# Six of 32 pieces of float64 weights narrowed during the retention, the other 26 with planned earliest times

## The chip, the core and the metric

The kernel runs on one core of a Trainium2 chip. The metric is the device time of one execution in microseconds (us). The engines are TensorE (PE, with its weight loads shown apart as PEld), VectorE (DVE), ScalarE (ACT), GpSimd (POOL) and SyncE (SP), which only issues transfers here. ACT and POOL issue some transfers too; their queues are named SPq, ACTq and POOLq.

## The reference

Three layers follow each other. Only what matters here is shown:

```python
scores = scale * np.matmul(q, k.transpose(0, 1, 3, 2))
ret = scores * Dmat[None, :, :, :]          # decays, causal
attn = np.matmul(ret, v)                    # 4 x 8 heads, 576 positions, 64 wide
# x: 2304 tokens x 512. 8 experts of 288 tokens each, filled in order of the logits
order = np.argsort(-flat)
h = np.maximum(x[mask] @ w1[e], 0.0)
out[mask] = h @ w2[e]
# last layer: 512 -> 2048 -> 512
h = x @ w_in
g = h * np.tanh(softplus(h))
return g @ w_out
```

`w_in` and `w_out` arrive as float64, since they are scaled by a float64 number. [...]

## The kernel before

**Retention (lines 133 to 304).** The 2304 tokens are worked through in 18 tiles of 128 (t = 0 to 17). In turn t of the loop at line 276 the program issues `load(t + 3)` (`qk` and `kv`, 512 KB each, line 168 and 170), `scale(t + 3)` on POOL (`ks`, `qs`, line 181 and 185), `scores(t + 1)` on PE (line 195) with its masking on DVE (`am`, line 198), then for tile t `carried` (line 223) and `outputs` (line 232) on PE into the PSUM tile `pT`, whose two halves ACT copies to `xT` (line 236), `state` (line 209, then DVE line 212), and `turn(t - 1)`: four matmuls into `pX` (line 246), a reduction on DVE (line 248), two ACT copies to `xs` (line 250) and a store (line 252). `pT` and `pX` share one tag with two buffers (line 216 and 243). They alternate, so that all `pT` tiles lie in one buffer and all `pX` tiles in the other: `carried(t + 1)` can't begin before `xT(t)` is copied out, nor `turn(t)` before `xs(t - 1)` is. The order of PE, DVE and POOL is that of the code (`manual_schedule`, line 147). The order of ACT and of SP's transfers in this part is chosen by the framework's scheduler. Loads have five buffers each.

**Routing and experts (lines 376 to 858).** Eight rounds follow. In each, DVE and PE find the 288 tokens of one expert bit by bit (`G`, `small`, lines 434 to 477), POOL gathers their rows (`xg`, line 613), PE transposes them (`mmx`, line 634), ACT and DVE split them into a high and a low part (`xh`, `xl`), and PE multiplies (`mma` and `mmb`, line 777). The weights come through five staging buffers (`st`) and are split likewise (`whi` on ACT, line 564; `wlo` on POOL or DVE, line 567). All this is recorded by a planner of the kernel's own (`run_tasks`, line 675): each task names an engine, a guessed duration, the events that it waits for and a priority (a smaller number goes first), and the planner writes the instructions down in the order in which they would start by its guesses.

**Narrowing (lines 705 to 767).** It is one of these planned tasks. There are 32 pieces (n = 0 to 31, 16 each of `w_in` and `w_out`), each of 128 x 512 float64 words (512 KB). Piece n is loaded into `std`; ACT scales the high words into `words` (line 741); DVE shifts (line 743) and joins low and high words into `dw` (line 746); ACT takes the sign into `dt` (line 750) and issues the store of piece n - 1 and the load of piece n + 3; POOL multiplies by the sign (line 760). Its priority is that of line 642: low (4) as long as the pieces are ahead of a plan that begins at `START` and allows `PACE` ns each, high (`UP`, 1.5) when they are behind it or when the eighth expert's tokens have been asked for (`URGENT`).

**Last layer (lines 860 to 1079).** The narrowed weights are read back (`final_units`), and six tiles of 384 tokens go through `hidden` (`mmc`, line 999), `gate` (sigmoid on ACT, two products and a reciprocal `q` on DVE, line 1029) and `outer` (`po`, line 1060).

Of the kernel before, what the change touches and what calls it, by code (L numbers as in the profile page):

```python
# [7 lines left out]
F32 = mybir.dt.float32  # L8
# [3 lines left out]
U32 = mybir.dt.uint32  # L12
# [13 lines left out]
NT = N // P  # L26
HP = H // 2
WARM = 11
STRADDLE = (4, 13)

GB = 96
# [21 lines left out]
NARROW_AT = (0, 0)  # L53
FIRST_UNITS = 2
EID = -2
PACE = 8000
START = 50000
WARM_TOOK = 215
WARM_N = 512
WARM_FROM = "tokens"  # L60
# [68 lines left out]
class Kernel:  # L129
# [3 lines left out]
    def attention(self):  # L133
# [8 lines left out]
        with ExitStack() as st:  # L142
            ld = st.enter_context(tc.tile_pool(name="ld", bufs=5))
            wk = st.enter_context(tc.tile_pool(name="wk", bufs=3))
            one = st.enter_context(tc.tile_pool(name="one", bufs=1))
            ps = st.enter_context(tc.tile_pool(name="ps", bufs=1, space=PSUM))
            st.enter_context(tc.manual_schedule(engines={mybir.EngineType.PE, mybir.EngineType.DVE, mybir.EngineType.Pool}))
            dec = one.tile([P, DCN], F32, name="dec")
# [26 lines left out]
            def scale(t, eng):  # L175

                if t >= NT:
                    return
                if not starts(t + 1):
                    KS[t] = wk.tile([P, H, D], F32, name="ks")  # L180
                    eng.tensor_tensor(KS[t], KV[t][:, 0], gks[:, t, :, None].to_broadcast([P, H, D]), op=ALU.mult)
                if not starts(t):
                    n = 64 if t in STRADDLE else P
                    QS[t] = QZ[t] if t in STRADDLE else wk.tile([P, HP, P], F32, name="qs")
                    eng.tensor_tensor(QS[t][:, :, :n], QK[t][:, 0, :, :n], gqs.rearrange("p (h i) -> p h i", i=P)[:, :, :n], op=ALU.mult)

            def scores(t):
                if t >= NT:
                    return
                pA = [ps.tile([P, HP, P], F32, name=f"pA{i}", tag="pA", bufs=2) for i in range(2)]  # L190
                for hp in range(HP):
                    for i in range(2):
                        sl = slice(i * 64, i * 64 + 64)
                        for o in (slice(0, 64), slice(64, P)):
                            nc.tensor.matmul(pA[i][o, hp, :], QK[t][sl, 1, hp, o], QK[t][sl, 0, hp, :], start=True, stop=True)
                AM[t] = wk.tile([P, 2, HP, P], F32, name="am")
                for i in range(2):
                    nc.vector.tensor_tensor(AM[t][:, i], pA[i], masks[t in STRADDLE][:, i], op=ALU.mult)

# [76 lines left out]
            for t in range(NT - 1):  # L276
                load(t + 3)
                scale(t + 3, nc.gpsimd)
                scores(t + 1)
                carried(t, Sb[seen[0] % 2])  # L280
                outputs(t)
                state(t)
                turn(t - 1)
                if t == 6:
                    self.routing_consts()
            t = NT - 1
            carried(t, Sb[seen[0] % 2])
            outputs(t)
            turn(t - 1)
            self.psum = lambda name, shape: ps.tile(shape, F32, name=name, tag="pS" if name == "pF" else "pA", bufs=1 if name == "pF" else 2)  # L290
            G = self.marks_of()
            self.chosen = self.rw.tile([GB, E, 3], I32, name="chosen", bufs=1)
# [346 lines left out]
        self.tasks.append([next(task), task])  # L639

    def narrow_priority(self):
        return UP if len(self.features) >= URGENT or len(self.narrowed) * PACE + START < self.time.get(PE, 0) else 4

    def arrival(self, n, at, wait=DMA_WAIT):
        self.time["dma"] = max(self.time.get("dma", 0), at.t) + n / DMA_RATE
# [53 lines left out]
    def step(self, t, done):  # L699
        try:  # L700
            t[0] = t[1].send(done)
        except StopIteration:
            self.tasks.remove(t)

    def narrow(self):

        nc, v, ic, a = self.nc, self.nc.vector, self.ic, self.a
        done = {k: {} for k in ("load", "read", "turn", "shift", "sign", "store")}

        def at(k, n):  # L710
            return [lambda: done[k].get(n)] if n >= 0 else []

        name = ("w_in", "w_out")
        words, sent = {}, {}

        def place(n):
            c, r = divmod(n // 2, a[name[n % 2]].shape[0] // P)
            return name[n % 2], slice(r * P, r * P + P), c

        def fetch(n, queue):  # L720
            if n < 32:
                w, r, c = place(n)
                words[n] = self.conv.tile([P, 512, 2], U32, name="std", bufs=3)
                queue.dma_start(words[n].rearrange("p c w -> p (c w)"), a[w].bitcast(U32)[r, c * 1024:c * 1024 + 1024])

        def send(n, queue):
            if n >= 0:
                w, r, c = place(n)
                queue.dma_start(a[w + "32"][r, c * 512:c * 512 + 512], sent.pop(n))

        def load():
            now = yield SP, 3 * DMA_ISSUE, [Event(0)], self.narrow_priority
            for n in range(3):
                fetch(n, nc.sync)
                self.spawn(piece(n, self.arrival(524288, now, LATE)))

        def piece(n, now):
            st, w = words[n], self.words.bitcast(U32)
            high = st[:, :, 1].bitcast(F32)
            now = yield ACT, 680, [now, *at("shift", n - 1)], self.narrow_priority  # L740
            nc.scalar.activation(self.words, high, AF.Copy, scale=2.0 ** -112)
            now = yield DVE, 620, [now], self.narrow_priority
            v.tensor_scalar(w, w, ic[:, IC["three"]], None, op0=ALU.logical_shift_left)
            now = yield DVE, 680, [now, *at("store", n - 4)], self.narrow_priority
            out = self.conv.tile([P, 512], U32, name="dw", bufs=4)
            v.scalar_tensor_tensor(out, st[:, :, 0], ic[:, IC["low"]], w, op0=ALU.logical_shift_right, op1=ALU.bitwise_or)
            done["shift"][n] = now
            sign = yield ACT, 800, [now, *at("sign", n - 1), *at("turn", n - 1)], self.narrow_priority
            t = self.conv.tile([P, 512], F32, name="dt", bufs=1)
            nc.scalar.sign(t, high)  # L750
            done["turn"][n] = sign
            send(n - 1, nc.scalar)
            fetch(n + 3, nc.scalar)
            if n:
                self.narrowed[n - 1] = done["store"][n - 1] = self.arrival(262144, sign, LATE)
            if n + 3 < 32:
                self.spawn(piece(n + 3, self.arrival(524288, sign, LATE)))
            now = yield POOL, 1310, [now, sign], self.narrow_priority
            sent[n] = out = out.bitcast(F32)
            nc.gpsimd.tensor_tensor(out, out, t, op=ALU.mult)  # L760
            done["sign"][n] = now
            if n == 31:
                now = yield SP, DMA_ISSUE, [now], self.narrow_priority
                send(n, nc.sync)
                self.narrowed[n] = self.arrival(262144, now)

        self.spawn(load())
# [354 lines left out]
```

## Time and profile before

| | |
|---|---|
| median of 3 runs | 800.22 us (799.56 to 802.0) |
| the profiled execution | 795.55 us, its span 793.8 us |
| PE busy | 752.2 us (95%) |
| PEld busy | 680.9 us (86%) |
| DVE, ACT, POOL busy | 670.7 (84%), 407.9 (51%), 484.1 us (61%) |
| moved by DMA | 112.53 MB, 142 GB/s mean |

A time is that of a whole execution; the span is the stretch of the profiled one in which instructions ran, and times in the rows below count from its start. Busy shares are means over stages with different limits: the retention ends at about 84 us, the experts at about 362 us, the last layer with the span.

### The profile page before, as it was taken

The numbers are of one execution on the slowest core, as the hardware profiler recorded it, in microseconds if no ns is written. First come the engines' busy times: TensorE is split into PE (matmuls) and PEld (weight loads), VectorE is DVE, ScalarE is ACT, GpSimd is POOL, SyncE is SP. The second block draws the span as 40 slices with busy tenths as digits, with TensorE's granted clock in tenths as the row PEclk, the third lists the DMA queues.
The fourth block names the chain that finished last, engine by engine and source line by source line (L and its number), as shares of the span: only waits on it lengthen the run. The fifth ranks groups of instructions, "written<-read, shape, count | busy, mean of one in ns | idle before, by whom it ended". The sixth has DMA issues, their size and how long they took to land.

```text
span 793.8 us, 16149 instructions
## 1 busy us (share of the span) xinstructions
PE 752.2 (95%) x6180; PEld 680.9 (86%) x6184; DVE 670.7 (84%) x1079; ACT 407.9 (51%) x781; POOL 484.1 (61%) x408
## 2 busy tenths in 40 slices
PE   6999469999999999799999999999999999999996
PEld 5888338999998999799999889789989989988995
DVE  2444687889889898777999999999999998999993
ACT  1233114557566575757765544564555555555452
POOL 5644035679797797430577565666657566666554
PEclk9999779999999999999999999999999999999999
DMA  9994156889888898986500010010001001000001
GB/s 341 408 338 156 54 172 204 268 286 305 268 285 297 277 308 252 349 287 205 178 20 21 1 46 15 21 40 21 13 8 51 10 20 41 21 1 22 19 1 40
DMA packets 61261, 112.53 MB, mean 142 GB/s; under 512 B 4864, under 2 KB 33152, under 8 KB 61184
## 3 DMA queue, kind: packets, MB, share of 16 engines
q1 hardware_dynamic: 44960, 74.01, 27.0%
q10 hardware_dynamic: 13248, 28.06, 10.3%
q0 software_dynamic: 2976, 9.44, 3.6%
q8 instruction: 48, 0.79, 0.4%
q14 instruction: 29, 0.24, 0.1%
HBM read 88.94 MB, written 22.54 MB: 140 GB/s over the span
## 4 chain that ended last, share of the span: by engine, by line
PE 42%; DVE 15%; ACT 2%; DMA 2%; POOL 2%; issue 1%; POOLq 0%; ACTq 0%; SPq 0%; DVEq 0%
PE po L1060 18%; PE mmc L999 17%; DVE q L1029 8%; PE mma L777 4%; DVE n L1024 4%; PE mmb L777 3%; DVE n L1034 1%; DMA st<-w 1%; ACT whi L564 1%; POOL n L1031 1%; DMA yt<-y_scratch 1%; DVE wlo L567 1%; POOL gl L1041 1%; POOL yl L959 0%; ACT q L1020 0%
## 5 line engine op out<-in xcount | busy, mean ns | idle before, releaser
L1029 DVE RECIPROCAL q<-q 128x384 f32<-128x384 f32 x96 | 243.9, 2541 | 4.7 <-ACT q L1027 4.6
L1031 POOL TENSOR_TENSOR n<-n,q 128x384 f32<-128x384 f32 x96 | 100.9, 1051 | 164.9 <-DVE q L1029 152.2
L567 POOL TENSOR_TENSOR wlo<-st,whi 128x1024 fp32r<-128x1024 f32 x51 | 122.7, 2419 | 15.7 <-ACT whi L564 11.6
L999 PE MATMUL mmc<-yl,whi 128*128 128x384 f32 x384 | 130.0, 338 | 2.1 <-POOL yl L959 2.0
L999 PE MATMUL mmc<-yh,whi 128*128 128x384 f32 x384 | 130.5, 340 | 0.1
L999 PE MATMUL mmc<-yh,wlo 128*128 128x384 f32 x384 | 129.9, 338 | 0.0
L1041 POOL TENSOR_TENSOR gl<-n,gh 128x384 fp32r<-128x384 f32 x96 | 118.6, 1239 | 7.0 <-ACT gh L1039 6.9
L1024 DVE SCALAR_TENSOR_TENSOR n<-s 128x384 f32<-128x384 f32 x96 | 113.6, 1184 | 3.7 <-POOL gl L1041 3.5
L1060 PE MATMUL po<-wlo,gh 128*128 128x512 f32 x288 | 115.6, 401 | 0.0
L1060 PE MATMUL po<-whi,gh 128*128 128x512 f32 x288 | 115.0, 399 | 0.0
L1060 PE MATMUL po<-whi,gl 128*128 128x512 f32 x288 | 114.0, 396 | 0.3 <-POOL gl L1041 0.3
L1039 ACT CAST gh<-n 128x384 fp32r<-128x384 f32 x96 | 49.3, 514 | 122.3 <-DVE n L1034 111.7
L564 ACT CAST whi<-st 128x1024 fp32r<-128x1024 f32 x80 | 82.9, 1045 | 33.8 <-DMA st<-w 27.8
L777 PE MATMUL mma<-xh,whi 128*128 128x288 f32 x256 | 78.0, 305 | 3.4 <-ACT xh L624 2.6
L777 PE MATMUL mma<-xl,whi 128*128 128x288 f32 x256 | 76.9, 301 | 1.9 <-DVE xl L626 1.9
L999 PEld LDWEIGHTS mmc<-yl,whi 128*128 128x128 f32 x384 | 72.1, 188 | 7.0 <-POOL yl L959 2.6
L777 PE MATMUL mmb<-hl,whi 128*128 128x288 f32 x256 | 77.3, 302 | 0.0
L777 PE MATMUL mmb<-hh,whi 128*128 128x288 f32 x256 | 77.2, 302 | 0.0
L777 PE MATMUL mma<-xh,wlo 128*128 128x288 f32 x256 | 76.6, 299 | 0.0
L999 PEld LDWEIGHTS mmc<-yh,whi 128*128 128x128 f32 x384 | 72.1, 188 | 4.8 <-ACT yh L956 0.3
L777 PE MATMUL mmb<-hh,wlo 128*128 128x288 f32 x256 | 75.8, 296 | 0.0
L999 PEld LDWEIGHTS mmc<-yh,wlo 128*128 128x128 f32 x384 | 72.0, 187 | 0.0
(149 smaller groups left out, 1522.3 us busy)
## 6 DMA issues: line engine op xcount, KB each, us to landing
st<-w SPq DMA_DIRECT2D x64, 512.0 KB, 6.1
qk<-qk SPq DMA_DIRECT2D x18, 512.0 KB, 8.1
kv<-kv SPq DMA_DIRECT2D x18, 512.0 KB, 6.6
std<-w_out ACTq DMA_DIRECT2D x15, 512.0 KB, 5.4
std<-w_in ACTq DMA_DIRECT2D x14, 512.0 KB, 5.4
x_scratch<-xs SPq DMA_DIRECT2D x18, 256.0 KB, 4.5
y_scratch<-y ACTq DMA_DIRECT2D x32, 144.0 KB, 4.3
yt<-y_scratch SPq DMA_DIRECT2D x22, 192.0 KB, 2.4
```

The lines of the kernel that those rows point to most:

```text
L564: self.nc.scalar.copy(dst[0], st)
L567: (self.nc.vector if lo.engine == DVE else self.nc.gpsimd).tensor_tensor(dst[1], st, dst[0].bitcast(F32), op=ALU.subtract)
L777: self.nc.tensor.matmul(bank[1][:, :CAP], al if h == 2 else ah, bl if h == 1 else bh, start=(first and j == h == 0), stop=(last and j == n ...
L999: self.nc.tensor.matmul(bank[1][:, :TILE], (wl if h == 2 else wh)[:, c, cs], x[c][h == 1], start=(c == h == 0), stop=(c == HP - 1 and h == 2))
L1024: v.scalar_tensor_tensor(u, s, 2.0, s, op0=ALU.subtract, op1=ALU.mult)
L1029: v.reciprocal(q, q)
L1031: nc.gpsimd.tensor_tensor(u, u, q, op=ALU.mult)
L1034: v.tensor_tensor(u, u, p, op=ALU.mult)
L1039: nc.scalar.copy(gh, u)
L1041: nc.gpsimd.tensor_tensor(gl, u, gh.bitcast(F32), op=ALU.subtract)
L1060: nc.tensor.matmul(po[j], (gl if h == 2 else gh)[:, js], (wl if h == 1 else wh)[:, f % 2], start=(f == h == 0), stop=(f == DFF // P - 1 an ...
```

## The change

Six pieces leave the planned narrowing and are written into the loop of the retention, in four steps per piece: its load, its shift (ACT, then DVE), its join (DVE, ACT for the sign, POOL for the product) and its store. By the code, piece n is loaded in turn n + 8, shifted in turn n + 10, joined in turn n + 11 and stored in turn n + 12. They have a pool of their own (`early`), in which `est`, the loaded piece, has three buffers and lies in SBUF as `ewords` does. The other 26 pieces stay in the planner, with a pace of 12000 instead of 8000 and a start at 45000 instead of 50000, and each now has an earliest planned time as well, which falls away with the eighth expert's request.

```diff
@@ constants
+EARLY_PIECES = 6
+PIECES_AT = 10
...
-PACE = 8000
-START = 50000
+PACE = 12000
+START = 45000
@@ attention
             one = st.enter_context(tc.tile_pool(name="one", bufs=1))
+            load_piece, shift_piece, join_piece, store_piece = self.early_pieces(st.enter_context(tc.tile_pool(name="early", bufs=1)))
...
             for t in range(NT - 1):
                 load(t + 3)
                 scale(t + 3, nc.gpsimd)
+                load_piece(t - PIECES_AT + 2)
                 scores(t + 1)
+                join_piece(t - PIECES_AT - 1)
                 carried(t, Sb[seen[0] % 2])
                 outputs(t)
                 state(t)
                 turn(t - 1)
+                shift_piece(t - PIECES_AT)
+                store_piece(t - PIECES_AT - 2)
...
             turn(t - 1)
+            for n in range(t - PIECES_AT - 2, EARLY_PIECES):
+                store_piece(n)
@@ narrow_priority
-        return UP if len(self.features) >= URGENT or len(self.narrowed) * PACE + START < self.time.get(PE, 0) else 4
+        return UP if len(self.features) >= URGENT or (len(self.narrowed) - EARLY_PIECES + 1) * PACE + START < self.time.get(PE, 0) else 4
@@ new
+    def early_pieces(self, pool):
+        nc, v = self.nc, self.nc.vector
+        st, words, out = {}, {}, {}
+        def load(n):
+            st[n] = pool.tile([P, 512, 2], U32, name="est", bufs=3)
+            nc.sync.dma_start(st[n].rearrange("p c w -> p (c w)"), self.piece_of(n)[0])
+        def shift(n):
+            words[n] = pool.tile([P, 512], F32, name="ewords", bufs=2)
+            nc.scalar.activation(words[n], st[n][:, :, 1].bitcast(F32), AF.Copy, scale=2.0 ** -112)
+            w = words[n].bitcast(U32)
+            v.tensor_scalar(w, w, self.ic[:, IC["three"]], None, op0=ALU.logical_shift_left)
+        def join(n):
+            out[n] = pool.tile([P, 512], U32, name="edw", bufs=3)
+            v.scalar_tensor_tensor(out[n], st[n][:, :, 0], self.ic[:, IC["low"]], words[n].bitcast(U32),
+                                   op0=ALU.logical_shift_right, op1=ALU.bitwise_or)
+            t = pool.tile([P, 512], F32, name="edt", bufs=2)
+            nc.scalar.sign(t, st[n][:, :, 1].bitcast(F32))
+            out[n] = out[n].bitcast(F32)
+            nc.gpsimd.tensor_tensor(out[n], out[n], t, op=ALU.mult)
+        def store(n):
+            nc.sync.dma_start(self.piece_of(n)[1], out[n])
...
@@ narrow
+        begin = EARLY_PIECES
+        for n in range(begin):
+            self.narrowed[n] = Event(0)
...
-            for n in range(3):
+            for n in range(begin, begin + 3):
...
         def piece(n, now):
...
-            now = yield ACT, 680, [now, *at("shift", n - 1)], self.narrow_priority
+            turn = lambda: Event(0 if len(self.features) >= URGENT else (n - begin) * PACE + START)
+            now = yield ACT, 680, [now, turn, *at("shift", n - 1)], self.narrow_priority
```

The instructions stand as follows. **ACT, start of the retention**, from the first `xT` on, before (tiles 0 and 1 make the `x4`):

```order
L236 COPY xT<-pT 128x256 x4
L250 COPY xs<-pX 128x4x64 x2
L236 COPY xT<-pT 128x256 x2
L250 COPY xs<-pX 128x4x64 x2
L236 COPY xT<-pT 128x256 x2
```

and with the change (lines 239 and 253 are the copies, 733 and 742 the two ACT steps of a piece):

```order
L239 COPY xT<-pT 128x256 x2
L733 ACTIVATE ewords<-est 128x512
L742 ACTIVATE edt<-est 128x512
L239 COPY xT<-pT 128x256 x2
L733 ACTIVATE ewords<-est 128x512
L742 ACTIVATE edt<-est 128x512
L253 COPY xs<-pX 128x4x64 x2
L239 COPY xT<-pT 128x256 x2
```

Both ACT steps of piece 0 now stand between the copies of tile 0 and of tile 1, and those of piece 1 ahead of the first `xs`. The ACT steps of pieces 2 to 5 stand much later, each ahead of an `xT` between tiles 11 and 14 or just behind it.

**SP, the transfers behind the fourth `kv`**, before (the `x2` are `qk` of tiles 5 and 6):

```order
L337 DMA rc<-rconsts 128x211
L339 DMA ic<-iconsts 128x194
L168 DMA qk<-qk 128x1024 x2
L170 DMA kv<-kv 128x1024
L168 DMA qk<-qk 128x1024
```

and with the change:

```order
L346 DMA rc<-rconsts 128x211
L348 DMA ic<-iconsts 128x194
L729 DMA est<-w_in 128x1024
L171 DMA qk<-qk 128x1024
L729 DMA est<-w_out 128x1024
L729 DMA est<-w_in 128x1024
L171 DMA qk<-qk 128x1024
L173 DMA kv<-kv 128x1024
```

The loads of pieces 0, 1 and 2 now lie among the first loads of the retention: piece 0 stands where `qk` of tile 5 stood, piece 1 where `kv` of tile 5 stood, and every later load is three places further back. The loads of pieces 3 to 5 stand behind the last `qk`.

**ACT, the transposed tokens of the seventh expert**, before (from the last but one `words` on):

```order
L741 ACTIVATE words<-std 128x512
L564 CAST whi<-st 128x1024
L811 COPY y<-mmb_5397 128x288
L813 DMA y_scratch<-y 128x288
L624 CAST xh<-mmx_5504 128x288
```

and with the change:

```order
L790 ACTIVATE words<-std 128x512
L573 CAST whi<-st 128x1024
L633 CAST xh<-mmx_5478 128x288
L633 CAST xh<-mmx_5483 128x288
L633 CAST xh<-mmx_5488 128x288
L633 CAST xh<-mmx_5493 128x288
L860 COPY y<-mmb_5383 128x288
```

The copy `y` and its transfer now stand behind the four `xh`. Counted over the whole of ACT's order, each of rounds 2 to 6 had five pieces before; now round 2 has four and rounds 3 to 6 have three. From round 7 on there were six left before, and there are nine now.

## Rows read from the trace of the kernel before

**Rows 1.** Stages (us: PE, PEld, DVE, ACT, POOL busy; granted clock; DMA share; GB/s).

```profile
14.00:84.00 70.00, 69.20 (x1433) 61.67 (x1430) 30.71 (x66) 22.05 (x68) 32.60 (x30) 0.99 0.79 297
140.00:310.00 170.00, 167.30 (x1773) 158.95 (x1773) 151.56 (x484) 102.58 (x175) 143.12 (x84) 1.00 0.85 285
310.00:330.00 20.00, 15.94 (x113) 15.26 (x112) 14.13 (x22) 14.53 (x35) 10.80 (x7) 0.91 0.95 324
330.00:362.00 32.00, 32.00 (x243) 32.00 (x242) 24.42 (x30) 19.63 (x34) 10.05 (x5) 1.00 0.73 249
505.00:782.00 277.00, 276.40 (x1360) 248.11 (x1361) 266.77 (x197) 147.67 (x284) 173.29 (x171) 0.99 0.06 21
```

**Rows 2.** Chain that ended last, last layer (start us, us, what).

```profile
510.66 2.12 PE mmc L999 x12
```

**Rows 3.** Timeline of PE, retention (start us, us, instruction).

```profile
20.05 0.62 PE L223 MATMUL pT<-qs,S 64*64 64x128 f32 x16
...
22.09 1.19 PE L246 MATMUL pX<-both,xT 128*128 128x136 f32 x8
...
39.81 1.19 PE L246 MATMUL pX<-both,xT 128*128 128x136 f32 x8
...
55.79 1.19 PE L246 MATMUL pX<-both,xT 128*128 128x136 f32 x8
...
59.88 1.19 PE L246 MATMUL pX<-both,xT 128*128 128x136 f32 x8
```

**Rows 4.** Timeline of ACT, retention (in brackets the idle time before).

```profile
17.66 0.65 ACT L236 COPY xT<-pT 128x256 f32<-128x256 f32 x2 [2.93 <-PE pT L232]
19.44 0.65 ACT L250 COPY xs<-pX 128x256 f32<-128x256 f32 x2 [1.14 <-DVE L L248]
```

**Rows 5.** Timeline of SP's queue, retention: `kv` 4, `qk` 5 and 6, `kv` 5.

```profile
12.99 0.43 SPq L170 DMA_DIRECT2D kv<-kv  x1
...
15.65 2.34 SPq L168 DMA_DIRECT2D qk<-qk  x2
18.94 0.33 SPq L170 DMA_DIRECT2D kv<-kv  x1
```

**Rows 6.** Timeline of POOL, retention: first use of `kv` 4 and `kv` 5.

```profile
22.88 1.04 POOL L181 TENSOR_TENSOR ks<-kv,dec 128x512 f32<-128x512 f32 x1 [0.29 <-DMA kv<-kv]
...
28.06 1.04 POOL L181 TENSOR_TENSOR ks<-kv,dec 128x512 f32<-128x512 f32 x1 [3.45 <-DMA kv<-kv]
```

**Rows 7.** Steps of a piece, by line (ns min/median/max, first and last start).

```profile
L741 ACT ACTIVATE words<-std x32: 625/642/677, 137.0 to 339.5; 128x512 f32<-128x512 f32 x32
L750 ACT ACTIVATE dt<-std x32: 657/672/717, 142.1 to 341.0; 128x512 f32<-128x512 f32 x32
L746 DVE SCALAR_TENSOR_TENSOR dw<-std,ic,words x32: 737/748/751, 144.7 to 344.1; 128x512 uint32<-128x512 uint32 x32
```

**Rows 8.** Stretches of 1 us, columns as in rows 1.

```profile
12.00:13.00 1.00, 1.00 (x14) 0.94 (x12) 0.86 (x2) 0.00 (x0) 0.72 (x1) 0.50 1.04 408
...
15.00:16.00 1.00, 1.00 (x36) 1.00 (x38) 0.36 (x1) 0.00 (x0) 0.36 (x1) 0.83 1.03 406
```

**Rows 9.** DMA issues from 55 to 75 us (count, size, median us to landing).

```profile
kv<-kv SPq DMA_DIRECT2D x3, 512.0 KB, 4.3
...
qk<-qk SPq DMA_DIRECT2D x2, 512.0 KB, 5.6
```

**Rows 10.** Timeline of PE, seventh expert's first matmuls.

```profile
320.40 0.40 PE L777 MATMUL mma<-xh,whi 128*128 128x288 f32 x1 [2.65 <-ACT xh L624]
```

**Rows 11.** Timeline of ACT, same place.

```profile
319.16 0.40 ACT L811 COPY y<-mmb 128x288 f32<-128x288 f32 x1
...
319.95 1.31 ACT L624 CAST xh<-mmx 128x288 fp32r<-128x288 f32 x4 [0.40 <-ACT y L811]
...
324.75 1.05 ACT L564 CAST whi<-st 128x1024 fp32r<-128x1024 f32 x1 [2.93 <-DMA st<-w]
325.70 0.40 ACT L800 ACTIVATE hh<-mma 128x288 fp32r<-128x288 f32 x1
```

More of the change, by code (lines that the diff above doesn't have):

```diff
@@ L703, in step, with piece_of, run @@
             self.tasks.remove(t)
+    def piece_of(self, n):
+        name = ("w_in", "w_out")[n % 2]
+        c, r = divmod(n // 2, self.a[name].shape[0] // P)
+        wide, narrow = self.a[name].bitcast(U32), self.a[name + "32"]
+        rows = slice(r * P, r * P + P)
+        return wide[rows, c * 1024:c * 1024 + 1024], narrow[rows, c * 512:c * 512 + 512]
+    def early_pieces(self, pool):
[19 more added lines that the diff above has]
+            nc.sync.dma_start(self.piece_of(n)[1], out[n])
+        def step(of):
+            def run(n):
+                if 0 <= n < EARLY_PIECES:
+                    of(n)
+            return run
+        return [step(x) for x in (load, shift, join, store)]
     def narrow(self):
@@ L708, in narrow @@
         done = {k: {} for k in ("load", "read", "turn", "shift", "sign", "store")}
+        begin = EARLY_PIECES
+        for n in range(begin):
+            self.narrowed[n] = Event(0)
         def at(k, n):
-            return [lambda: done[k].get(n)] if n >= 0 else []
-        name = ("w_in", "w_out")
+            return [lambda: done[k].get(n)] if n >= begin else []
         words, sent = {}, {}
-        def place(n):
-            c, r = divmod(n // 2, a[name[n % 2]].shape[0] // P)
-            return name[n % 2], slice(r * P, r * P + P), c
         def fetch(n, queue):
             if n < 32:
-                w, r, c = place(n)
                 words[n] = self.conv.tile([P, 512, 2], U32, name="std", bufs=3)
-                queue.dma_start(words[n].rearrange("p c w -> p (c w)"), a[w].bitcast(U32)[r, c * 1024:c * 1024 + 1024])
+                queue.dma_start(words[n].rearrange("p c w -> p (c w)"), self.piece_of(n)[0])
         def send(n, queue):
-            if n >= 0:
-                w, r, c = place(n)
-                queue.dma_start(a[w + "32"][r, c * 512:c * 512 + 512], sent.pop(n))
+            if n >= begin:
+                queue.dma_start(self.piece_of(n)[1], sent.pop(n))
         def load():
             now = yield SP, 3 * DMA_ISSUE, [Event(0)], self.narrow_priority
-            for n in range(3):
+            for n in range(begin, begin + 3):
                 fetch(n, nc.sync)
```

2 lines of the change are left out of this document (1 added, 1 removed).

## The prediction

> **What bounds the kernel now.** I read the table by stages first, then the chain of waits, then the timelines of the retention. The reader is to see in the stages [rows 1] that PE has work almost without a break in three of them: 69.20 of 70 us in the retention, 167.30 of 170 us in the rounds, 276.40 of 277 us in most of the last layer, where the chain runs over PE's matmuls [rows 2]. Only between 310 and 330 us, where the rounds end, is PE idle for 20 - 15.94 = 4.1 us, and its granted clock is 0.91 there. So work taken from DVE, ACT or POOL in the rounds can give back at most what PE idles there, and work put into the retention costs nothing as long as PE doesn't wait for it. That is the question to ask of the new order of ACT and SP.
>
> **The six pieces in the retention: PE is made to wait.** In busy time there is room: over the 70 us of the retention ACT works 22.05 us, DVE 30.71, POOL 32.60 [rows 1], and one piece brings ACT 0.64 + 0.67 = 1.31 us and DVE two steps of some 0.75 us [rows 7]. But the scheduler of ACT's order has put both ACT steps of piece 0 ahead of `xT(1)`, and those of piece 1 ahead of `xs(0)`. ACT takes its instructions in order, so `xT(1)` now waits for the landing of piece 0.
>
> When does that land? Its load takes the place that `qk` of tile 5 had, issued at 15.65 us [rows 5]. The neighbours took long, since the queue is full: `kv` of tile 4 was issued at 12.99 [rows 5] and POOL, idle, got it at 22.88 [rows 6], 9.9 us later; `kv` of tile 5 went from 18.94 to 28.06, 9.1 us. So piece 0 lands between 24.8 and 25.6; I take 25.2. Piece 1 has the very place of `kv` of tile 5 and lands at 28.1.
>
> - `xT(1)`: 25.2 + 1.31 for the two steps [rows 7] = 26.5, and 0.65 for the two copies [rows 4]: ready at 27.2 instead of 17.66 + 0.65 = 18.3. `carried(2)` on PE needs the buffer of `pT(1)`, so it begins at 27.2 instead of 20.05 [rows 3]: 7.1 us late.
> - `xs(0)`: 28.1 + 1.31 + 0.65 = 30.05. `turn(1)` needs the buffer of `pX(0)` and begins at 30.05 instead of 22.09 [rows 3]: 8.0 us late.
> - PE has then been idle for some 7 us. [...] I take 8.6, the middle of 8.0 and 9.2.
>
> From there PE goes at its own pace again, so the delay stays. What can come back: from 22.09 to 39.81 four tiles took 4.43 us each, later ones 59.88 - 55.79 = 4.09 [rows 3]; if all of that excess is waiting for loads, which get a lead while PE stands still, 4 x 0.34 = 1.4 us return. What can come on top: the three later pieces are loaded only when a buffer is freed by the join of an earlier one, about 3 us into a turn of 4.1 us, and their ACT step stands ahead of an `xT` that PE needs two turns later. By the positions that leaves some 4.6 us for the landing, and loads took 4.3 to 5.6 us there [rows 9]: 0 to 1.0 us. I let 0.7 and 0.6 cancel: **the retention gets 8.5 us longer**, bounds 8.0 - 1.4 = 6.6 and 9.2 + 1.0 = 10.2. That three loads stand ahead of the others costs nothing more: three times 512 KB at the 408 GB/s of [rows 8] are 3.9 us, and the tiles that use those loads come 8 us later.
>
> [...]
>
> **Rounds 2 to 6.** By the order they go from 25 pieces to 16, which takes 9 x 1.5 = 13.5 us from DVE's 151.56 busy ones and 9 x 1.31 = 11.8 us from ACT's 102.58. But PE has only 170 - 167.30 = 2.7 us of idle there [rows 1]. The new order also puts a few matmuls of the old expert behind the transposes of the next, where PE waited for `xl`. I take **2.5 us back**, bounds 0 and 2.7.
>
> **The end of the rounds.** In the seventh expert `y` and its transfer now stand behind `xh`, for which PE waited 2.65 us [rows 10]: `xh` would begin at 319.16 instead of 319.95 [rows 11], **0.8 us back**. Against it, nine pieces instead of six have to be done here, 3 x 1.31 = 3.9 us more of ACT and 4.5 us of DVE. From 330 to 362 us ACT is idle for 12.4 us and DVE for 7.6 us [rows 1], which hides them; if that cover fails, the weights of the eighth expert come late and PE, which has no break there, waits. Bounds: all 4.1 us of PE's idle time between 310 and 330 back, or 3 us lost.
>
> Sum: 8.5 - 2.5 - 0.8 = +5.2 us. The profiled execution's 795.55 us would become 800.8; its place is 4.7 us under the median of the runs, and the change of a median should be the same: 800.22 + 5.2 = **805.4 us**.
>
> **Rivals.**
> 1. *The rounds have more room than PE's busy time shows* (faster). Ends of matmuls are modelled, and the weight loads are busy for only 158.95 of the 170 us [rows 1], so up to 11.05 us could be waiting. If all of it goes with the nine pieces: 8.5 - 11.05 - 0.8 = -3.4, 796.9 us. It decides from 7.7 us of return on. Against it: those gaps also hold the many short routing matmuls, and only 9 of 25 pieces leave; their share of the gaps, 9/25 x 11.05 = 4.0, gives 803.9, still slower. [...] Together with the case that ACT isn't held up (8.5 becomes 0: 796.9 as well), chance 0.08.
> 2. *A short delay and a good end* (same). Retention at its lower bound 6.6, rounds 2.7, and half of PE's idle time at the rounds' end, 2.0: +1.9, 802.1 us. For it: the excess of the first tiles does look like waiting for loads. Chance 0.18.
> 3. *The nine late pieces get in the way* (slower still). They have priority over the eighth expert's weights; +3 us at the end instead of -0.8, retention at 10.2: 810.9 us. The transfers are already at 0.95 of their time between 310 and 330 us [rows 1]. Chance 0.12.
>
> That the change doesn't quite do what its words say (the first two pieces meet the first tiles, not the last, and nine of 26 aren't spread) is read from the order and lies in the forecast already, which has 0.62. A measurement of this kernel can tell about 0.3%, 2.4 us, from no change; so faster is below 797.8, slower above 802.6. Faster 0.08, same 0.18, slower 0.74. The range goes from 799.5, just under the sum of all favourable bounds (6.6 - 2.7 - 4.1 = -0.2, 800.0 us), to 810.5, where the retention is at its upper bound and nothing comes back (10.2, 810.4 us).
>
> **What would show it.** In the profile after: ACT idle until about 25 us, its idle time ended by the transfer of `est`; the second `xT` near 26.5 instead of 17.66; a break of 7 us on PE ahead of `carried(2)`, a granted clock of 0.50 behind it; the first routing step some 8 us later than before; rounds shorter by half a microsecond each. The forecast is wrong if `est` lands well ahead of 24 us, or if the rounds from the first gather to the last get shorter by over 5 us.

## The result, and the profile after

The change makes the kernel slower, by a little over 1%: 809.21 us in the median of 6 runs (808.14 to 810.01), where the kernel before takes 799.71 us (6 runs, 799.39 to 802.0). The ratio is 1.0117, with a 95% interval of 1.0105 to 1.0128, so 8.4 to 10.2 us. The profiled execution took 809.21 us, with a span of 807.4 us.

The stages of the profile after, cut where the same work lies (columns and order as in [rows 1]: retention, rounds, end of the rounds, the stretch behind it, last layer):

```profile
14.00:94.00 80.00, 70.92 (x1415) 63.19 (x1408) 41.76 (x79) 28.23 (x78) 40.42 (x35) 0.94 0.87 317
150.00:320.00 170.00, 163.02 (x1729) 155.00 (x1728) 138.87 (x462) 90.21 (x155) 130.91 (x74) 1.00 0.73 239
320.00:342.00 22.00, 19.95 (x168) 19.20 (x168) 17.39 (x27) 15.88 (x36) 8.83 (x8) 1.00 0.89 313
342.00:374.00 32.00, 32.00 (x242) 32.00 (x242) 28.33 (x37) 25.91 (x42) 13.98 (x8) 1.00 0.98 336
515.00:792.00 277.00, 275.07 (x1356) 247.10 (x1355) 267.56 (x199) 149.15 (x288) 173.13 (x171) 0.99 0.06 21
```

The retention takes some 10 us more and PE stands still for 80 - 70.92 = 9.1 us of it, where it had stood still for 0.8. In the rounds DVE has lost 12.7 us of work and ACT 12.4 (13.5 and 11.8 were worked out ahead), and PE stands still for 7.0 us of these 170 instead of 2.7; in a second profile of the kernel before (experiment 1) it is 6.3. The stretch behind the rounds now has its transfers at 0.98 of their time instead of 0.73.

ACT's timeline after, at the place of [rows 4]:

```profile
24.50 0.66 ACT L733 ACTIVATE ewords<-est 128x512 f32<-128x512 f32 x1 [11.47 <-DMA est<-w_in]
25.06 0.65 ACT L742 ACTIVATE edt<-est 128x512 f32<-128x512 f32 x1
25.60 0.64 ACT L239 COPY xT<-pT 128x256 f32<-128x256 f32 x2
27.05 0.67 ACT L733 ACTIVATE ewords<-est 128x512 f32<-128x512 f32 x1 [0.81 <-DMA est<-w_out]
...
28.18 0.62 ACT L253 COPY xs<-pX 128x256 f32<-128x256 f32 x2
```

PE's timeline after, at the place of [rows 3]:

```profile
26.34 1.13 PE L226 MATMUL pT<-qs,S 64*64 64x128 f32 x16 [6.36 <-issue]
30.16 2.09 PE L249 MATMUL pX<-both,xT 128*128 128x136 f32 x8
...
74.37 0.67 PE L226 MATMUL pT<-qz,S 64*64 64x128 f32 x16 [1.01 <-POOL qs L188]
```

And two stretches of PE after (busy, granted clock, DMA share, GB/s):

```profile
20.00:26.00 6.00, 0.00 (x0) 0.65 1.03 402
26.00:30.00 4.00, 3.66 (x48) 0.50 1.03 411
```

That is the forecast's first step: ACT idle until piece 0 has landed, the second `xT` at 25.60 (forecast 26.5), a break on PE ahead of `carried(2)`, and then the granted clock at 0.50, at which `turn(1)` takes 2.09 us instead of 1.19. The row of the break names no releaser (`issue`), but `carried(2)` begins at 26.34, 0.1 us behind the end of the second `xT`. The row at 74.37 is one that the forecast had only as a small term. It names POOL, but `qz` had been ready for 9 us; `carried(13)` needs the buffer that `xT(12)` empties, and ACT's timeline after shows what that waited for:

```profile
73.07 0.67 ACT L733 ACTIVATE ewords<-est 128x512 f32<-128x512 f32 x1 [1.39 <-DMA est<-w_out]
73.64 0.63 ACT L239 COPY xT<-pT 128x256 f32<-128x256 f32 x2
...
77.40 0.68 ACT L733 ACTIVATE ewords<-est 128x512 f32<-128x512 f32 x1 [1.38 <-DMA est<-w_in]
77.99 0.62 ACT L239 COPY xT<-pT 128x256 f32<-128x256 f32 x2
```

`xT(12)` ends at 74.27 and `carried(13)` begins at 74.37. It is the same queue again, with the late pieces.

How late a tile is can be read from DVE's reduction of its `L`. The second, the ninth and the last one, in before_again (experiment 1) and then in the change:

```profile
23.11 0.17 DVE L248 TENSOR_REDUCE L<-pX 128x8 f32<-128x16 f32 x1 [0.69 <-PE pX L246]
52.18 0.17 DVE L248 TENSOR_REDUCE L<-pX 128x8 f32<-128x16 f32 x1 [0.69 <-PE pX L246]
86.38 0.17 DVE L248 TENSOR_REDUCE L<-pX 128x8 f32<-128x16 f32 x1
```

```profile
32.28 0.17 DVE L251 TENSOR_REDUCE L<-pX 128x8 f32<-128x16 f32 x1 [1.58 <-PE pX L249]
60.11 0.17 DVE L251 TENSOR_REDUCE L<-pX 128x8 f32<-128x16 f32 x1 [0.69 <-PE pX L249]
96.59 0.17 DVE L251 TENSOR_REDUCE L<-pX 128x8 f32<-128x16 f32 x1
```

### The profile page after: what moved, and what is told of

The parts are those of the page before. It is cut to its first block, busy times and chain, and to the rows that moved or that the text cites. A ratio compares the mean times of both kernels' runs of the same rounds, so it can differ in the third digit from the quotient of the medians.

```text
span 807.4 us, 16152 instructions
## 1 busy us (share of the span) xinstructions
PE 753.7 (93%) x6180; PEld 680.9 (84%) x6184; DVE 674.3 (84%) x1079; ACT 408.0 (51%) x781; POOL 484.3 (60%) x408
## 4 chain that ended last, share of the span: by engine, by line
PE 44%; DVE 16%; ACT 3%; issue 1%; DMA 1%; POOL 1%; ACTq 1%; POOLq 0%; SPq 0%; DVEq 0%
PE po L1109 17%; PE mmc L1048 17%; DVE q L1078 8%; PE mma L826 5%; PE mmb L826 4%; DVE n L1073 4%; DVE n L1083 1%; ACT whi L573 1%; DMA q<-y_scratch 1%; DVE wlo L576 1%; PE small L461 1%; DMA y_scratch<-y 1%; DVE G L443 1%; POOL gl L1090 0%; POOL n L1080 0%
```

## Experiments

All runs side by side. "Last tile" is the start of the last reduction of `L` on DVE, which ends the retention. "Rounds" is from the first to the seventh gather `xg`. "Left" is the number of pieces (of the float64 weights that are turned into float32) whose first ACT step comes after the eighth gather. "End" is from the eighth gather to the 13th reciprocal of the last layer. The ratio is that to the kernel before, run beside it, with its 95% interval. All stages are of one profiled execution each; the first two rows, one program twice, show how far two executions can lie apart.

| run | median us | ratio | last tile | rounds | left | end |
|---|---|---|---|---|---|---|
| before, as predicted from | 799.71 | | 87.13 | 192.79 | 6 | 120.61 |
| before_again | 799.85 | 1.0004 (0.9993 to 1.0014) | 86.38 | 197.23 | 6 | 119.77 |
| the change | 809.21 | 1.0117 (1.0105 to 1.0128) | 96.59 | 195.32 | 9 | 121.23 |
| scalar_by_code | 802.21 | 1.0027 (1.0016 to 1.0039) | 90.42 | 195.13 | 9 | 120.17 |
| old_plan | 807.82 | 1.0097 (1.0066 to 1.0128) | 99.49 | 197.76 | 0 | 115.48 |
| scalar_by_code_old_plan | 799.28 | 0.9994 (0.9983 to 1.0006) | 90.00 | 198.81 | 0 | 115.56 |
| transfers_by_code | 817.33 | 1.0225 (1.0200 to 1.0251) | 105.43 | 195.37 | 9 | 119.81 |
| more_y_buffers | 809.43 | 1.0114 (1.0084 to 1.0144) | 96.95 | 195.07 | 9 | 122.26 |
| staged_old_plan | 795.48 | 0.9947 (0.9932 to 0.9961) | 86.23 | 198.35 | 0 | 116.36 |
| staged_new_plan | 799.06 | 0.9981 (0.9969 to 0.9993) | 86.32 | 195.57 | 9 | 121.16 |
| seven_staged | 798.43 | 0.9975 (0.9955 to 0.9996) | 90.70 | 197.86 | 0 | 115.58 |

**1. before_again: the kernel before, once more.** Against the first profile the rounds of the change had become 2.5 us longer, with fewer pieces in them. Either the new order cost that, or the first profile was an odd one.

> The kernel before, once more, for a second profile of it. The profiled execution of before took 795.55 us while its timed runs gather at 799.7, and the traces differ by 13.6 us of span where the medians differ by 9.5. If that profile was an odd one, this one has a span near 797.5 to 798, and the stage that is some 4 us longer shows where the profiled execution of before was lucky. If a profile of this kernel is always shorter than its timed runs, the span is near 794 again.

Its span is 796.9 us, and the rounds are where it differs: 197.23 us against 192.79. The odd execution was the one that the prediction was read from. The difference lies in DVE's wait for the routing's result; the same two instructions at the same place of the fourth round, in the trace of before (first pair, PE and DVE) and of before_again (second pair):

```profile
210.71 0.17 PE L457 MATMUL small<-sat,digit 128*128 128x8 bf16 x1 [0.27 <-DVE sat L373]
210.91 0.17 DVE L418 TENSOR_REDUCE sc<-small 128x1 uint32<-128x8 f32 x1 [0.26 <-PE small L457]
```

```profile
211.77 0.17 PE L457 MATMUL small<-sat,digit 128*128 128x8 bf16 x1 [0.27 <-DVE sat L373]
212.47 0.17 DVE L418 TENSOR_REDUCE sc<-small 128x1 uint32<-128x8 f32 x1 [0.76 <-PE small L457]
```

The reduction begins 0.20 us after the matmul's start in the one and 0.70 us after it in the other, with the same neighbours. So what the change does in the rounds is to be read against before_again.

**2. scalar_by_code: is it ScalarE's queue?** One edit, which puts ACT's instructions of the retention in the order of the code (here and in experiment 5 the names of the engines are shortened):

```diff
-manual_schedule(engines={PE, DVE, Pool})
+manual_schedule(engines={PE, DVE, Pool, Activation})
```

> The change with one edit: ScalarE's instructions in the retention stand in the order of the code, so both ScalarE steps of piece n stand behind the xs copies of tile n+9; the three early loads stay where they were on the transfer queue. Theory 1 (ScalarE's queue held by the steps of pieces 0 and 1): the first outputs' copies go at once, carried(2) starts near 20 instead of 26.3, the 7.2 us that are left of the delay at tile 8 go, and the time falls by 6 to 7.5 us to 801.7 to 803.2; the stalls at tiles 13 and 15 stay, with 1.5 to 2.5 us. Theory 2 (the three early loads take the transfer bandwidth from the tiles' loads): carried(2) stays at 24 or later or the tiles 3 to 5 wait for their qk and kv, at least 4 us of the delay are left, and the time is 805 or more. The rounds keep their 33.15 us in either.

802.21 us, 7.0 less than the change, inside what theory 1 gave. PE's timeline of scalar_by_code, at the place of [rows 3]:

```profile
19.64 0.64 PE L226 MATMUL pT<-qs,S 64*64 64x128 f32 x16
21.71 1.19 PE L249 MATMUL pX<-both,xT 128*128 128x136 f32 x8
```

The break is gone, although the three early loads stand where they stood: the loads cost PE nothing there, the order of ACT's steps does. At the ninth tile the retention is as good as on time (`L` at 52.87 us, 52.18 in before_again). Then it falls back by 3.3 us more, to 90.42, where theory 1 had 1.5 to 2.5 us left from ACT's stalls. DVE's timeline of scalar_by_code points at another queue (L735 is the shift of a piece, L739 the join, L215 the state that `carried` needs):

```profile
58.45 0.49 DVE L735 TENSOR_SCALAR ewords<-ewords,ic 128x512 uint32<-128x512 uint32 x1 [1.33 <-ACT ewords L733]
58.86 1.28 DVE L201 TENSOR_TENSOR am<-pA,mask 128x512 f32<-128x512 f32 x2
...
60.05 1.55 DVE L739 SCALAR_TENSOR_TENSOR edw<-est,ic,ewords 128x512 uint32<-128x512 uint32 x1
61.53 0.41 DVE L215 TENSOR_TENSOR S<-pS,dec 128x256 f32<-128x256 f32 x1
```

DVE waits 1.33 us for ACT's step of the same piece, and the join, which takes 1.55 us, stands ahead of the state. Whether that is the cause, experiments 7 to 9 test.

**3 and 4. old_plan and scalar_by_code_old_plan: what the new plan does.** The early pieces stay; the other 26 are planned as before:

```diff
-PACE = 12000
-START = 45000
+PACE = 8000
+START = 50000
...
-            turn = lambda: Event(0 if len(self.features) >= URGENT else (n - begin) * PACE + START)
-            now = yield ACT, 680, [now, turn, *at("shift", n - 1)], self.narrow_priority
+            now = yield ACT, 680, [now, *at("shift", n - 1)], self.narrow_priority
```

(and without the + 1 in `narrow_priority`.) The second run has the edit of run 2 as well.

> The change with six pieces early as it has them, but the other 26 planned as before: no earliest time, and the old pace and start. The order in the rounds is then the order of before, with five pieces a round and one or two left for the end. Theory 1 (the new order, in which an expert's rounding step stands between the two comparisons of a round's choice on VectorE, makes each round 0.54 us longer): the gathers of the rounds lie 32.4 to 32.65 us apart instead of 33.15, the retention is as late as in the change (first gather near 121.5), and with the stall of 2.7 us in the shared expert, which needs late transfers, gone as well the time falls by 2.6 to 6 us, to 803 to 806.6. Theory 2 (the rounds are longer for another reason, such as a transfer or a clock that the early pieces shift): the gathers stay 33.1 apart and the time stays at 808 or more.

> Both edits: ScalarE's retention order by the code, and the other 26 pieces planned as before. If the two losses are separate, they add: 809.2 less 6 to 7.5 less 2.6 to 6, 796 to 800.6, beside 799.7 of the kernel before; what the six pieces then cost is the stalls at tiles 13 and 15 (some 2 us), and what they bring is the end of the rounds. If they are not separate, because the rounds' end is bound by something else once the retention is on time, the time is over 801.

Both theories of old_plan fell: with the order of before the gathers of the second to the sixth round lie 33.4 to 33.6 us apart, neither 32.4 to 32.65 nor 33.1, and the rounds are longer than with the new plan, 197.76 and 198.81 against 195.32 and 195.13. Behind them it is the other way round: with the old plan no piece is left for after the eighth gather, and the end takes 115.5 us instead of 120.2 to 121.2. Part of both differences is work that changes sides at the seventh gather, as shown further down. The time of old_plan, 807.82 us, spreads from 803.68 to 811.19; its profiled execution shows how that can be. Timeline of ACT, timeline of PE and two stretches of PE (busy, granted clock, DMA share, GB/s) of old_plan:

```profile
73.89 0.67 ACT L733 ACTIVATE ewords<-est 128x512 f32<-128x512 f32 x1 [2.49 <-DVE am L201]
74.47 0.62 ACT L239 COPY xT<-pT 128x256 f32<-128x256 f32 x2
```

```profile
75.20 0.77 PE L226 MATMUL pT<-qz,S 64*64 64x128 f32 x16 [2.11 <-POOL edw L744]
```

```profile
74.00:76.00 2.00, 0.80 (x18) 0.91 1.01 333
76.00:80.00 4.00, 4.00 (x37) 0.50 0.91 326
```

(The first row names DVE's `am`, which this step doesn't use; the load of its piece was issued at 66.92 us, 7.0 us ahead of it.) `xT(12)` comes 0.8 us later than in the change, PE's break is 2.11 us instead of 1.01, and behind the longer one the granted clock is 0.50 (from 76 to 80 us). The last tile comes 2.9 us later than in the change, though nothing in the retention's order differs. With ScalarE by the code no break there is over 1.1 us, and 799.28 us, inside the 796 to 800.6 for two separate losses, is no different from the kernel before: against before_again 3.6 us are lost in the retention and 1.6 in the rounds, and 4.2 gained at the end.

**5. transfers_by_code: is it enough that the loads come late?** SyncE instead of Activation in the list of run 2:

```diff
-manual_schedule(engines={PE, DVE, Pool})
+manual_schedule(engines={PE, DVE, Pool, SP})
```

> The change with SyncE's transfers of the retention in the order of the code instead of ScalarE's instructions: the loads of the first three pieces then stand behind the tiles' loads of tiles 11 to 13 and no longer behind that of tile 4, and the scheduler, which placed ScalarE's steps by these loads, now places the steps of pieces 0 and 1 behind the copies of tiles 9 and later by itself. Theory 1 (the delay at tile 2 is the wait of ScalarE's queue for an early load, wherever it comes from): carried(2) starts near 20, the time falls by 5 to 8 us, to 801 to 804, as with ScalarE by the code. Theory 2 (it is the place of ScalarE's steps alone, and late loads bring the same wait back at tiles 9 to 12, where the transfers are still busy): carried(2) is on time, but ScalarE waits over 1 us for a piece's load ahead of a tile's copy at two or more of the tiles 9 to 14, and the time is 804 to 808.

817.33 us, slower than either theory had it. DVE's third state is on time (21.86 us, 21.99 in before_again), so late loads do away with the first break; but theory 2 is right that they bring back the wait, and larger. ACT's timeline of transfers_by_code:

```profile
55.43 0.69 ACT L733 ACTIVATE ewords<-est 128x512 f32<-128x512 f32 x1 [2.69 <-DMA est<-w_in]
...
61.91 0.68 ACT L733 ACTIVATE ewords<-est 128x512 f32<-128x512 f32 x1 [4.14 <-DMA est<-w_out]
...
67.61 0.67 ACT L733 ACTIVATE ewords<-est 128x512 f32<-128x512 f32 x1 [3.38 <-DMA est<-w_in]
```

The edit also moved the load of the routing's constants behind the tiles of its turn, and DVE waited 5.1 us for it once; that part has nothing to do with the pieces, so the size of this run is not all theirs.

**6. more_y_buffers: what breaks PE in the last layer?** In the profile after, ACT waits for the store of an earlier `y`, and from 402.3 us on PE stands still (timelines of ACT and of PE):

```profile
393.15 0.40 ACT L860 COPY y<-mmb 128x288 f32<-128x288 f32 x1 [3.12 <-DMA y_scratch<-y]
```

```profile
405.03 0.44 PE L1048 MATMUL mmc<-yh,whi 128*128 128x384 f32 x1 [2.74 <-DVE n L1083]
```

The edit gives `y` one buffer more, at the cost of one of the narrowed pieces:

```diff
-y = self.fa.tile([P, CAP], F32, name="y", bufs=YB)
+y = self.fa.tile([P, CAP], F32, name="y", bufs=YB + 1)
...
-out = self.conv.tile([P, 512], U32, name="dw", bufs=4)
+out = self.conv.tile([P, 512], U32, name="dw", bufs=3)
```

> The change with four buffers instead of three for the rounded results that ScalarE copies out, and three instead of four for the narrowed pieces to make room; every engine's order is the same. Theory 1 (the break of 2.7 us in the shared expert near 402 us comes from ScalarE waiting 3.1 us for an earlier store of results to land, which the late pieces' transfers hold up): that wait goes or falls under 1 us, TensorE's break goes, and the time falls by 2 to 3.4 us, to 805.8 to 807.2. Theory 2 (the break is bound by VectorE's work in that stretch, the wait only its neighbour): the break stays over 2 us and the time stays at 808.5 or more. One buffer less for the narrowed pieces may cost a wait of a round's later piece on its store; that would show as ScalarE or VectorE waiting for a store of dw in the rounds.

Half of theory 1 came true: ACT no longer waits for a store there, and the break shrinks. PE's timeline of more_y_buffers:

```profile
383.17 0.44 PE L1048 MATMUL mmc<-yh,whi 128*128 128x384 f32 x1 [1.39 <-ACT yh L1005]
...
406.13 0.44 PE L1048 MATMUL mmc<-yh,whi 128*128 128x384 f32 x1 [1.09 <-DVE n L1083]
```

But the first of these rows comes 61.25 us after the eighth gather, not 58.56, and the time does not change (809.43 us): what is gained behind it is lost ahead of it. There the granted clock was 0.83 from 10 to 20 us behind the gather, 1.00 in the change; staged_new_plan has 0.83 there too, without this edit. In the five profiles with nine pieces left the break goes with ACT's wait for that store: waits of 3.12, 2.79, 2.02, 1.98 us and none, breaks of 2.74, 2.43, 1.66, 1.57 and 1.09 us; none of the other six profiles has a break there. So the wait makes part of the break, not all of it, and what it costs in time this run doesn't show.

**7 to 9. The staged pieces.** If DVE's queue is what is left in the retention, each step of a piece should stand one tile behind the one that it needs, and the join behind the state:

```diff
-                load_piece(t - PIECES_AT + 2)
+                load_piece(t - PIECES_AT + 1)
                 scores(t + 1)
-                join_piece(t - PIECES_AT - 1)
                 carried(t, Sb[seen[0] % 2])
                 outputs(t)
                 state(t)
+                join_piece(t - PIECES_AT - 2)
                 turn(t - 1)
-                shift_piece(t - PIECES_AT)
-                store_piece(t - PIECES_AT - 2)
+                shift_piece(t - PIECES_AT - 1)
+                words_piece(t - PIECES_AT)
+                store_piece(t - PIECES_AT - 3)
...
```

`words_piece` holds both ACT steps, `PIECES_AT` is 9, `ewords` and `edt` have three buffers, ACT stands by the code. With the old plan:

> Six early pieces, the other 26 planned as before, ScalarE by the code, and each early piece spread over four tiles: both ScalarE steps behind the xs copies of one tile, VectorE's shift behind the reduction of the next, its join behind the state of the tile after that, so that VectorE never waits for ScalarE in between and the state goes ahead of the join. With both edits but without this the retention's last turn ended 3.6 us behind that of the kernel before (90.00 against 86.38), with VectorE waiting 1.3 us for ScalarE at each of six tiles. Theory 1 (VectorE's queue: that wait, and the join ahead of the state): the last turn comes at 86.4 to 88, 2 to 3.6 us earlier, and the time is 795.7 to 797.3, 2.4 to 4 us under the kernel before. Theory 2 (the two engines that share the work of a piece slow each other, VectorE's 0.73 us of a join becoming 1.55 to 1.81 beside GpSimd): the last turn stays at 89 or later, and the time is 798.3 or more.

795.48 us, 4.5 us under the kernel before beside it (ratio 0.9947, interval 0.9932 to 0.9961), and 13.7 under the change. The last tile is at 86.23 us, no later than in before_again: six pieces in the retention cost nothing. DVE's timeline of staged_old_plan (L740 shift, L744 join):

```profile
56.08 0.78 DVE L740 TENSOR_SCALAR ewords<-ewords,ic 128x512 uint32<-128x512 uint32 x1
...
58.98 0.42 DVE L215 TENSOR_TENSOR S<-pS,dec 128x256 f32<-128x256 f32 x1 [0.67 <-PE pS L212]
59.33 1.35 DVE L744 SCALAR_TENSOR_TENSOR edw<-est,ic,ewords 128x512 uint32<-128x512 uint32 x1
```

The join still takes 1.35 us, but behind the state, where nothing waits for it; so theory 2, that the sharing of the work itself costs the time, fell, and the place of the steps in the queues was the cause. The same pieces with the change's plan:

> The early pieces staged over four tiles as in staged_old_plan, with the change's own plan of the other 26. Theory 1 (the parts are separate, and the new plan gains some 2.8 us in the rounds and loses 4.6 at the eighth expert and the shared expert's start): the last turn comes within 0.7 us of staged_old_plan's 86.23, the first to the seventh gather take 195.1 to 195.4 us, from the eighth gather to the thirteenth reciprocal 119.5 to 121.5 us pass where staged_old_plan has 116.4, and the time is 797 to 799, beside 795.5. Theory 2 (with the retention on time the loss at the end is hidden): that stretch takes under 118 us and the time is under 796.

799.06 us, at the edge of what theory 1 gave; the stages are near it (last tile 86.32, rounds 195.57, end 121.16). The retention's part is separate from the plan's, and the new plan costs 3.6 us net by the medians, 2.7 by the ratios to the kernel before beside each. And one piece more:

> Seven early pieces instead of six, one tile earlier, staged and with the old plan: the rounds then take the other 25 in five times five, and none is left for the stretch after the last gather. Theory 1 (each piece less after the last gather frees transfers there): from the eighth gather to the thirteenth reciprocal 115 to 116.3 us, the last turn up to 0.7 us later for the seventh piece, and the time 794.5 to 795.8. Theory 2 (that stretch no longer waits for transfers with one piece left, and the seventh piece only costs in the retention, where the transfers are busy until 60 us): the time is 796 or more.

798.43 us. The end was already free of pieces with six, so there was little more to gain (115.58 against 116.36), and the retention lost 4.5 us; one tile took 7.84 us from reduction to reduction there, 4.09 in before_again. ACT's timeline of seven_staged there:

```profile
70.32 0.67 ACT L734 ACTIVATE ewords<-est 128x512 f32<-128x512 f32 x1 [3.91 <-DMA est<-w_in]
```

A piece loaded late, its ACT step ahead of a tile's copy: the first mechanism once more. Theory 2 was right.

## Why the prediction was right, and where its sum failed

The direction and its main cause were right: the change is slower because ACT's queue is held in the retention, and run 2, which changes only that order, gives back 7.0 us. The size was not. The forecast was +5.2 us and the median moved by 9.5; between the executions of the change and of before_again the difference is 10.5 us. Of that the retention has 10.2, where 8.5 had been taken, and all that lies behind it 0.3, where -3.3 had been taken. Term by term this is nearly the third rival (10.2 - 2.5 + 3, chance 0.12). The range held because its upper end was drawn for the retention at its upper bound with nothing coming back, and that is what happened.

**The retention: forecast +8.5, measured +10.2** (96.59 against 86.38 for the last tile), at the upper bound.
- The first step has the forecast's upper case, 9.2 us (32.28 - 23.11 at the second reduction), but partly by luck in its parts. No run shows the forecast's way to its 9.2, and so to the 8.6 that it took: that was the author's estimate. What the change shows in its place is 3.82 us from the start of `carried(2)` to that of `turn(1)` (26.34 and 30.16), at a granted clock of 0.50, where [rows 3] have 2.04. ACT kept to its order here: `xT(1)` began at 25.60, behind both steps of piece 0, though the matmuls into its `pT` had ended by 16.21. Piece 0 was ready for ACT at 24.50 where 25.2 had been taken, and `carried(2)` was 6.5 us late, not 7.1 (26.34 against 19.81 in before_again). The granted clock of 0.50 lasted until 32 us (0.99 from 32 to 33) and took 1.75 us between `carried(2)` and `turn(1)` and 0.9 us in `turn(1)`, which the forecast had left out. `xs(0)` was ready at 28.80, ahead of `turn(1)` at 30.16, so the forecast's other path, that of the 8.0 us, did not decide.
- What came back was 1.2 us (at the ninth tile the delay is 60.11 - 52.18 = 7.9), near the 1.4 that had been the most; 0.7 had been taken.
- "0 to 1.0 us" for the three later pieces was the first term that failed: 2.3 us were lost there. The mechanism was the right one, but its price was set once, for one piece. Three pieces come in turn, each ahead of the copy of a tile: the tiles' reductions lie 5.47, 4.73 and 4.48 us apart there (72.36, 77.83, 82.56, 87.04) instead of 4.08, which is 1.39 + 0.65 + 0.40 = 2.4. The first load took 67.20 to 73.07, 5.9 us, just above the 4.3 to 5.6 of [rows 9].

**The rounds: forecast -2.5, measured -1.9, but not in the forecast's way.** From the first to the seventh gather it is 195.32 us against 197.23 in before_again. Over the five programs with three or four pieces a round (195.07 to 195.57) and the other plans of five (197.23 to 198.81, the odd execution left aside) it is between -1.7 and -3.7. The forecast let this come out of PE's idle time, of which the odd execution had 2.7 us in 170. These two stretches, in the change and in before_again (columns as in [rows 1]):

```profile
121.46:316.78 195.32, 184.31 (x1958) 171.80 (x1961) 158.50 (x535) 100.48 (x172) 146.28 (x81) 1.00 0.72 238
```

```profile
111.23:308.46 197.23, 187.14 (x1973) 173.33 (x1972) 169.94 (x554) 112.74 (x193) 158.20 (x89) 1.00 0.82 273
```

PE idles no less: 11.0 us against 10.1 (10.1 to 11.1 over the five programs, 10.1 to 10.8 over the other plans of five). What is less is its work. One of the three groups of matmuls into `mmb` in these stretches, in the change and in before_again:

```profile
L826 PE MATMUL mmb<-hh,whi 128*128 128x288 f32 x160 | 48.9, 306 | 0.0
```

```profile
L777 PE MATMUL mmb<-hh,whi 128*128 128x288 f32 x164 | 49.9, 304 | 0.0
```

All three groups have 160 instead of 164, in every profile with the new plan: twelve matmuls stand behind the seventh gather. They follow each other every 0.13 us (the change, from 316.91 us on), which makes 1.6 us of work put off, not saved. The forecast had seen these matmuls move and had counted it as a gain. So this term was right in size by luck; neither PE's idle time nor the 11.05 us of the weight loads' idle time, the first rival's, was had. Read against the profile that the prediction had, the rounds seem 2.5 us longer; that is the difference of experiment 1, not of the change.

**The end of the rounds: forecast -0.8, measured +2.2.** From the seventh gather to the last store it is 802.15 - 316.78 = 485.37 us, in before_again 791.58 - 308.46 = 483.12. Up to 1.6 us of that are the twelve matmuls. Rounds and end together, from the first gather to the last store, take 680.69 us against 680.35: +0.3, and the forecast return of 3.3 us did not come. The 0.8 us were there: in the 20 us behind the eighth gather PE idles 2.0 us instead of 3.8. Nor did the cover of ACT and DVE fail in the stretch for which it was claimed: PE works 32.00 of the 32 us from 342 us on. But it was looked for only that far, and PE's break of 2.74 us lies behind it, ahead of 405.03 us. Stretches behind the eighth gather, in the change (first two) and at the same distance from it in staged_old_plan (last two), columns as in [rows 1]:

```profile
361.85:371.85 10.00, 10.00 (x78) 10.00 (x77) 9.36 (x13) 8.08 (x14) 2.15 (x1) 1.00 0.92 309
371.85:381.85 10.00, 9.57 (x69) 9.08 (x68) 6.19 (x10) 4.86 (x10) 0.00 (x0) 1.00 1.03 351
```

```profile
354.33:364.33 10.00, 10.00 (x77) 10.00 (x76) 5.01 (x8) 5.28 (x9) 0.00 (x0) 1.00 0.09 19
364.33:374.33 10.00, 10.00 (x71) 9.61 (x70) 7.33 (x11) 6.54 (x10) 0.00 (x0) 1.00 0.94 318
```

With nine pieces left the transfers have no gap between 361.85 and 381.85 us; with none they are at 0.09 for ten of these twenty. The third rival had this ("the nine late pieces get in the way") and a price of 3 us. Over all runs the end takes 115.5 to 116.4 us with none left, 119.8 to 120.6 with six and 119.8 to 122.3 with nine. None against some is clear; six and nine overlap, and with nine some ten of the moved matmuls are in it too. From the first gather to the 13th reciprocal, which counts them once, it is 318.0 to 319.6 us with none, 320.3 to 322.4 with nine, and with six 321.8 in before_again and 318.2 in the odd execution. That is a count against a time. Whether the transfers, or the steps of these pieces on DVE and ACT, carry it was not taken apart by a run of its own.

So the six early pieces do bring what one hopes of them if the other 26 keep their old plan: 3.4 to 4.3 us at the end, 2.2 to 3.8 us with the rounds ahead of it. With the change's plan nine are left for the end, and from the first gather to the 13th reciprocal next to nothing of it remains (321.62 us against 321.84). The forecast priced each stage's relief, but not what a piece costs where it goes.

The last step, that "the change of a median should be the same" as that of the profiled execution, was safe for the retention and not for the rounds: the execution read from was 4.2 us under the median of its own kernel, and its rounds were 4.4 us shorter than those of before_again.

## What to carry to other kernels

An instruction that a scheduler puts early in an engine's order can be paid for by what stands behind it: here ACT was idle for 11.47 us ahead of piece 0's first step, and the order of the code gave 7.0 us back (run 2). Give side work that waits for a transfer a place on the queue behind the copies that free the main engine's buffers, one tile later for each engine that it passes through, and behind the step that the main engine waits for; and issue its load early enough (experiment 9). When such steps repeat, price each one, not the first alone. Work that is spread out of one stage has to be done in another: count what is left for the later stage before relaxing a plan. When a stage got shorter, count its instructions before calling it faster: some may only have crossed its border. Read a baseline from two profiled executions where a few microseconds matter.

## What the runs showed of the hardware

- One program, run twice, had rounds of 32.4 to 32.6 us in one execution and 33.4 to 33.5 in the other (the first and the last round aside), by up to 0.5 us more between a small matmul and the reduction of its result, at fixed places of the round. Of the eleven profiled executions ten show the first round at 32.35 to 32.37 us and one at 33.42, so it can change from round to round. Why the reduction starts late no row shows, and it stays open.
- A break of PE of 1.01 us at the 14th tile left the granted clock at 1.00 (the change); one of 2.11 us at the same place was followed by 0.50 (old_plan). 1.1 us more of waiting became 3.5 us more between two reductions (8.97 us against 5.47). A break of 2.74 us ahead of 405.03 us left the clock at 1.00 all the same (the change), so the length of the break alone does not tell.
- A piece's join on DVE takes 0.73 to 0.75 us alone and 1.0 to 1.8 us when it begins while POOL is at work. In all 25 such cases of the nine runs with early pieces it ended 0.54 to 0.56 us after POOL's instruction, however much of that was left. In the change these are the joins at 74.60 and 80.50 us, of 1.25 and 1.80 us, which end 0.55 us after POOL's `edw` (75.30) and `qs` (81.75). GpSimd's product took longer as well where it began during a join: a `ks` at 71.35 us in the change took 1.24 us (the join from 70.94 to 71.67), and 1.04 elsewhere. Why, no row shows.
- The row of a wait names the last releaser by the clock, which here was twice POOL where ACT's copy was meant; the time at which the copy ended, 0.1 us ahead of the matmul (74.27 and 74.37 us in the change, 75.09 and 75.20 in old_plan), tells the two apart.
